# Two decode layers on one core: two more cache units kept between the layers, six places for w2, one first transfer, a result of 128 rows

## The chip, the cores and the metric

One core of a Trainium2 chip runs the whole program. The metric is the device time of one execution in microseconds, the median of a few runs. The profile is one execution taken by the hardware profiler; its times count from the span's start.

## The reference

```python
def _A_ref(x, k_cache, v_cache, wq, wo):      # attention of one token, 32 heads, 4096 keys, head size 128
    q = (x @ wq).reshape(B, Sq, H, Dh)
    scores = einsum("bhqd,bhkd->bhqk", q, k_cache) * (Dh ** -0.5)
    p = softmax(scores)
    o = einsum("bhqk,bhkd->bhqd", p, v_cache)
    return o.reshape(B, Sq, H * Dh) @ wo
def _B_ref(x, w1, b1, w2, b2):                # 512 -> 1376 -> 512
    return gelu(x @ w1 + b1) @ w2 + b2
for _ in range(2):                            # the same weights and caches both times
    x = x + _A_ref(layernorm(x), k_cache, v_cache, wq, wo)
    x = x + _B_ref(layernorm(x), w1, b1, w2, b2)
```

Everything is float32. K and V are 64 MiB each, far more than the core's own memory, so each layer reads nearly all of them again.

## The kernel before

The 32 heads go in 8 groups of 4. A group's K is a block of 8 MiB (8 chunks of 1 MiB, `NC` = 2048 columns on 128 partitions), and so is its V. A unit `U` is 512 columns, 256 KB; four units make a chunk. Group g is written below as K0 to K7 and V0 to V7. Layer 0 takes the groups 0 to 7, layer 1 takes them 7 to 0, so K7 and V7 are still there when layer 1 begins, and so are parts of V6.

One tile, `arena`, holds everything that is loaded. Places in it are columns worked out by hand: three blocks in turn, then `SPARE` (8 units, over V6's chunks 5 and 6), `HELD` (w1), and `PAIR` (two chunks: a group's wo and the next group's wq). All loads are issued by SP through `load` (L85 to L88) in program order, one after the other; a load whose place is still read waits there, and all loads behind it wait too. The transfers themselves run in that order.

For each group: `queries` (L211) makes q from wq on VectorE and TensorE, `scores` (L230) are 32 products a group over K, `softmax` (L235) uses VectorE, ScalarE and TensorE, and V is weighted either by products on TensorE (`values`, L260) or on ScalarE and VectorE (`weighted_by_act`, `weighted`). `late_sum` and `late_out` put a group's last sums (L283) and its wo product (L309, L311) behind the fifth chunk of the next group's scores. `idle` (L437) is a product whose result nobody reads.

Between the layers stands `mlp` (L335). In layer 0 it multiplies with w2, eleven units, in eight places of `SPARE` (`W2_AT[0]`, c modulo 8). As products free the places, `follow` (L622 to L627) issues more loads from inside the loop at c = 3, 5, 7 and 9: the rest of w2, wq of group 6, and the first units of K6. The last quarter of that goes out at L637, and K6's second chunk at L451 in two halves, behind the products of `query_block` (L197) that read the place. In layer 1, n = 1 loads the rest of K6 over K7 as K7's chunks have been used (L480), then what of V6 is not there (L482); n = 1 also asks for six of K5's eight chunks over V7 and `SPARE` (L518).

Of V6, chunks 0 to 4 stay where they are, and six units more (`KEPT`) are saved in layer 0: five in PSUM (`pK`, copied at L540 and back at L484) and one in `pB` (L606, back at L506). n_kept at L481 is the first column of V6 that has to be loaded again.

Of the kernel before, what the change touches and what calls it, by code (L numbers as in the profile page):

```python
# [28 lines left out]
KEPT = 6  # L29

# [11 lines left out]
K2_HOME = 12 * NC  # L42

V1_HOME = *(2 * BLOCK + NC * c for c in range(5)), 8 * NC, 6 * NC, 7 * NC
W2_AT = tuple(SPARE + U * (c % 8) for c in range(FB)), tuple(U * c for c in range(FB))
# [15 lines left out]
def decode_layers(ctx: ExitStack, tc: tile.TileContext, k, v, w, w1, w2, out):  # L61
# [33 lines left out]

    def of_w(first, n):

        row, i = first
        return w[row][:, AHEAD + NC * i : AHEAD + NC * (i + n)]
# [7 lines left out]
    def free_now(layer, n):  # L107

        if layer == 0:
            at = HELD + 2 * NC  # L110
        elif n == 0:
            at = 6 * NC
            return arena[:, at : at + U], arena[:, 11 * NC : 11 * NC + 4 * 129]
        else:
            at = 9 * NC if n == 1 else 14 * NC
# [14 lines left out]
    row, _ = wq_at(0)  # L130
    ahead = load(HELD, w[row][:, : AHEAD + NC])
    wq_first = chunk(ahead[:, AHEAD:])

# [77 lines left out]
    def queries(n, xc, wt, at, t=None, short=False, between=None):  # L211
        t = wt[:, 0, :] if t is None else t
        pin(nc.vector.tensor_scalar(t, wt[:, 0, :], xc[:, 0:1], None, op0=ALU.mult))
        for c in range(1, 4):
            pin(nc.vector.scalar_tensor_tensor(t, wt[:, c, :], xc[:, c : c + 1], t, op0=ALU.mult, op1=ALU.add))  # L215
# [14 lines left out]
    def scores(z, c, kt):  # L230
        for j in range(J):
            pin(nc.tensor.matmul(pS[32 * j : 32 * j + C, :], z[:, j, C - 1 - c : 2 * C - 1 - c],  # L232
                                 kt[:, j, :], start=(c == 0), stop=(c == C - 1)))
# [206 lines left out]
    for layer in range(2):  # L440
# [9 lines left out]
        if layer == 1:  # L450
            for a in (0, NC // 2):  # L451
                load(PAIR + NC + a, part(k, order[1], 1, 2)[:, a : a + NC // 2])
            here["k", order[1], 1] = chunk(arena[:, PAIR + NC : PAIR + 2 * NC])
# [10 lines left out]
        for n, g in enumerate(order):  # L464
# [35 lines left out]
            if first or final:  # L500
                for _ in range(FILL if layer == 1 else 0):
# [51 lines left out]
            if layer == 1 and n == 0:  # L553
# [46 lines left out]
            if n == G - 2:  # L600

                row = arena[:, HELD - U : HELD] if layer == 0 else p
# [16 lines left out]
        if layer == 0:  # L619
            first_k, next_wq = part(k, G - 2, 0, 1), of_w(wq_at(G - 2), 1)  # L620
            follow = {
                3: (*((W2_AT[0][a], w2[:, U * a : U * b]) for a, b in W2_PARTS[0][3:]),  # L622
                    (SPARE + NC - U, first_k[:, NC - U :])),
                5: ((SPARE + NC, next_wq[:, : 2 * U]),),
                7: ((SPARE + NC + 2 * U, next_wq[:, 2 * U :]),),
                9: ((SPARE, first_k[:, : 2 * U]),),
            }  # L627
        mlp(x1, s1, w1_t, w2_t[layer], xb, *((None, last_v) if layer == 0 else (ends, None)), follow)
        if layer == 0:
# [4 lines left out]
            g = G - 2  # L634
            wq_first = wq_next
            wq_next = chunk(arena[:, SPARE + NC : SPARE + 2 * NC])
# [51 lines left out]
```

## Time and profile before

| | us |
|---|---|
| median of 3 runs | 673.32 |
| lowest and highest run | 673.31, 673.92 |
| the profiled execution: its span | 671.6 |
| the median run over that span | 1.7 |

| engine | busy us | share of the span |
|---|---|---|
| VectorE (DVE) | 407.1 | 61% |
| TensorE (PE) | 299.7 | 45% |
| ScalarE (ACT) | 215.4 | 32% |
| DMA engines, share of their time in the program's queue | | 99.1% |

The span runs from the first to the last instruction of the profiled execution. What the device's time has beyond it, 1.7 us here, is taken as the same for both kernels. The busy shares of the engines are means over stages that differ; the DMA engines are the one resource that is busy from end to end.

### The profile page before, as it was taken

The numbers are of one execution on the slowest core, as the hardware profiler recorded it, in microseconds if no ns is written. First come the engines' busy times: TensorE is split into PE (matmuls) and PEld (weight loads), VectorE is DVE, ScalarE is ACT, GpSimd is POOL, SyncE is SP. The second block draws the span as 40 slices with busy tenths as digits, with TensorE's granted clock in tenths as the row PEclk, the third lists the DMA queues.
The fourth block names the chain that finished last, engine by engine and source line by source line (L and its number), as shares of the span: only waits on it lengthen the run. The fifth ranks groups of instructions, "written<-read, shape, count | busy, mean of one in ns | idle before, by whom it ended". The sixth has DMA issues, their size and how long they took to land.

```text
span 671.6 us, 6013 instructions
## 1 busy us (share of the span) xinstructions
PE 299.7 (45%) x2236; PEld 79.7 (12%) x2236; DVE 407.1 (61%) x510; ACT 215.4 (32%) x697; POOL 5.2 (1%) x26
## 2 busy tenths in 40 slices
PE   1511703415116053165768986704316025065597
PEld 1000100101001010011114311101001001011124
DVE  3059679498696886971322313288597694973513
ACT  0047074190560823802011200083290650910010
POOL 1000000000000000000000000000000000000000
PEclk9965755757558557578689998655757559557799
DMA  9999999999999999999999999999999999999997
GB/s 377 437 437 438 435 437 437 403 461 437 437 437 397 444 426 434 433 429 426 425 415 399 422 422 438 437 433 433 431 433 437 437 430 402 462 426 414 431 414 286
DMA packets 11556, 285.29 MB, mean 425 GB/s; under 512 B 1284, under 2 KB 1288, under 8 KB 3720
## 3 DMA queue, kind: packets, MB, share of 16 engines
q1 hardware_dynamic: 11528, 284.92, 99.1%
q8 instruction: 17, 0.28, 0.2%
q14 instruction: 11, 0.09, 0.0%
HBM read 284.92 MB, written 0.00 MB: 424 GB/s over the span
## 4 chain that ended last, share of the span: by engine, by line
DMA 64%; PE 17%; DVE 15%; issue 1%; another core or an unknown queue 1%; SPq 1%; ACT 0%; DVEq 0%; ACTq 0%
DMA arena<-in_v 37%; DMA arena<-in_k 24%; PE pS L232 8%; DVE arena L274 7%; PE pO L262 5%; DMA arena<-in_w 4%; DVE arena L279 3%; DVE arena L311 2%; PE pO L283 1%; DVE arena L287 1%; DVE arena L215 1%; SPq L87 1%; PE pB L323 1%; DVE arena L309 0%
## 5 line engine op out<-in xcount | busy, mean ns | idle before, releaser
L269 ACT ACTIVATE arena<-arena,pt 128x128 f32<-128x128 f32 x640 | 188.0, 387 | 50.8 <-DMA arena<-in_v 48.1
L232 PE MATMUL pS<-arena,smalls 128*8 128x512 f32 x1024 | 147.0, 727 | 78.4 <-DMA arena<-in_k 74.3
L279 DVE TENSOR_TENSOR arena<-arena 128x4096 f32<-128x4096 f32 x30 | 132.6, 4420 | 0.3
L274 DVE TENSOR_TENSOR arena<-arena,pt 128x2048 f32<-128x2048 f32 x40 | 89.0, 2287 | 36.8 <-DMA arena<-in_v 35.7
L217 PE MATMUL pS<-arena,smalls 128*128 128x512 f32 x20 | 20.7, 1140 | 202.5 <-DVE arena L215 202.5
L244 ACT ACTIVATE arena<-pS,smalls 128x512 f32<-128x512 f32 x16 | 12.4, 777 | 289.4 <-DVE smalls L243 289.4
L287 DVE STREAM_TRANSPOSE arena<-pO 128x512 f32<-128x512 f32 x16 | 11.5, 717 | 97.4 <-PE pO L262 61.9
L262 PE MATMUL pO<-arena,pt 128*4 128x512 f32 x368 | 48.9, 666 | 11.8 <-DMA arena<-in_v 11.0
L232 PEld LDWEIGHTS pS<-arena,smalls 128*8 128x8 f32 x1024 | 29.8, 102 | 198.6 <-issue 177.3
L236 DVE TENSOR_REDUCE smalls<-pS 128x1 f32<-128x512 f32 x16 | 11.0, 687 | 64.1 <-PE pS L232 64.1
L215 DVE SCALAR_TENSOR_TENSOR arena<-arena,smalls 128x512 f32<-128x512 f32 x45 | 33.8, 752 | 1.6
L311 DVE SCALAR_TENSOR_TENSOR arena<-arena,smalls 128x512 f32<-128x512 f32 x39 | 29.3, 752 | 1.4
L217 PEld LDWEIGHTS pS<-arena,smalls 128*128 128x128 f32 x20 | 5.0, 311 | 206.2 <-DVE arena L215 206.2
L315 PE MATMUL pB<-arena,smalls 128*1 128x512 f32 x26 | 14.7, 648 | 29.0 <-DVE arena L311 29.0
L246 PE MATMUL pO<-ident,arena 128*128 128x128 f32 x64 | 13.4, 344 | 28.1 <-ACT arena L244 27.8
L574 DVE TENSOR_TENSOR arena<-arena 128x2048 f32<-128x2048 f32 x10 | 22.9, 2292 | 0.3
L382 ACT ACTIVATE smalls<-smalls 128x4 f32<-128x4 f32 (+1 forms) x6 | 1.2, 205 | 44.0 <-DVE smalls L375 25.6
L262 PEld LDWEIGHTS pO<-arena,pt 128*4 128x4 f32 x368 | 9.8, 93 | 44.8 <-issue 42.4
L250 DVE STREAM_TRANSPOSE smalls<-smalls 128x32 f32<-128x32 f32 x16 | 3.4, 212 | 17.5 <-ACT arena L244 17.5
L246 PEld LDWEIGHTS pO<-ident,arena 128*128 128x128 f32 x64 | 8.4, 167 | 42.1 <-ACT arena L244 36.7
L244 ACT ACT_TABLE_LOAD x1 | 1.3, 1283 | 36.9 <-DVE smalls L243 36.9
L438 PE MATMUL pS<-arena,ident 128*8 128x256 f32 (+1 forms) x34 | 11.9, 454 | 0.5 <-DVE pt L367 0.5
(115 smaller groups left out, 183.6 us busy)
## 6 DMA issues: line engine op xcount, KB each, us to landing
arena<-in_w SPq DMA_DIRECT2D x13, 2048.0 KB, 12.5
arena<-in_k SPq DMA_DIRECT2D x6, 4096.0 KB, 21.3
arena<-in_v SPq DMA_DIRECT2D x2, 4096.0 KB, 25.1
arena<-in_w SPq DMA_DIRECT2D x6, 1024.0 KB, 30.9
arena<-in_v SPq DMA_DIRECT2D x2, 2048.0 KB, 37.0
arena<-in_k SPq DMA_DIRECT2D x2, 2048.0 KB, 13.4
arena<-in_w SPq DMA_DIRECT2D x7, 512.0 KB, 9.3
arena<-in_v SPq DMA_DIRECT2D x3, 1024.0 KB, 46.3
```

The costliest lines, as they stand in the source:

```text
L215: pin(nc.vector.scalar_tensor_tensor(t, wt[:, c, :], xc[:, c : c + 1], t, op0=ALU.mult, op1=ALU.add))
L217: pin(nc.tensor.matmul(at, one.to_broadcast([P, P]), t, start=True, stop=True))
L232: pin(nc.tensor.matmul(pS[32 * j : 32 * j + C, :], z[:, j, C - 1 - c : 2 * C - 1 - c], kt[:, j, :], start=(c == 0), stop=(c == C - 1)))
L246: nc.tensor.transpose(pT[:, b].rearrange("p j r -> p (j r)"), p[:, P * b : P * (b + 1)], ident)
L262: nc.tensor.matmul(pO[32 * j : 32 * j + 4, :], pt[:, j, c, :], by_head(vt)[:, j], start=(i == 0), stop=(i == of - 1))
L269: nc.scalar.activation(own, own, AF.Copy, scale=pt[:, j, c, b : b + 1])
L274: nc.vector.tensor_tensor(own, own, weight, op=ALU.mult)
L279: pin(nc.vector.tensor_tensor(a, a, b, op=ALU.add))
L287: nc.vector.transpose(ot[:, :512], pO)
L311: pin(nc.vector.scalar_tensor_tensor(t, wt[:, d, :], on[:, d : d + 1], t, op0=ALU.mult, op1=ALU.add))
L315: pin(nc.tensor.matmul(pB[0:1, :], one, t, start=n == 0, stop=n == G - 2))
L574: pin(nc.vector.tensor_tensor(total, total, other, op=ALU.add))
```

## The change

- Two units more of V6 stay (`INPLACE` = 2): the last two of chunk 6, at `SPARE` + 6 and + 7 units, are not overwritten, so the load at L482 starts 512 KB later in V6. Chunk 6's first two units, which were saved in PSUM, come back to `SPARE` + 4 and + 5 units (`V1_HOME`), where all four then lie side by side.
- For that, w2 in layer 0 has six places (c modulo 6). Its parts (6, 8), (8, 10) and (10, 11) all go out from `follow`. The row of pB lies in the fifth place, and so part (4, 6), and w1's last part behind it, wait for the products that read the row (L332).
- wq of group 6 goes to the places 5, 0, 1 and 4 as four units; K6's first two units to the places 2 and 3, its next four to `PAIR` in one load, and the rest over K7 (units 6 to 10, 10 to 14, 14 to 32).
- K5's first six chunks go in one load over V7 (`K2_HOME` = 10 chunks), and `SPARE` is not needed for them.
- x, biases, wq of group 0, wo of group 0 and wq of group 1 come in one first load from an array of their own, where wo and wq of group 1 were a load behind V0.
- The result is written as 128 rows of 512 bytes instead of 4; the host takes every 32nd.
- In layer 0's last group, three idle products follow the scores and two the softmax, as they do in layer 1.

```diff
+INPLACE = 2
-K2_HOME = 12 * NC
-V1_HOME = *(2 * BLOCK + NC * c for c in range(5)), 8 * NC, 6 * NC, 7 * NC
-W2_AT = tuple(SPARE + U * (c % 8) for c in range(FB)), tuple(U * c for c in range(FB))
+K2_HOME = 10 * NC
+V1_HOME = *(2 * BLOCK + NC * c for c in range(5)), 8 * NC, SPARE + NC, 7 * NC
+W2_AT = tuple(SPARE + U * (c % 6) for c in range(FB)), tuple(U * c for c in range(FB))
...
+    def unit(t, j):
+        return t[j] if isinstance(t, list) else t[:, j, :]
+    def units(*places):
+        return [arena[:, at : at + U] for at in places]
...
         elif n == 0:
-            at = 6 * NC
-            return arena[:, at : at + U], arena[:, 11 * NC : 11 * NC + 4 * 129]
+            at, ot_at = 6 * NC + 2 * U, 9 * NC + 3 * U - 4
+            return arena[:, at : at + U], arena[:, ot_at : ot_at + 4 * 129]
...
-    row, _ = wq_at(0)
-    ahead = load(HELD, w[row][:, : AHEAD + NC])
+    ahead = load(PAIR - AHEAD - NC, start)
     wq_first = chunk(ahead[:, AHEAD:])
+    w_first = chunk(ahead[:, AHEAD + NC :]), chunk(ahead[:, AHEAD + 2 * NC :])
...
-        if layer == 1:
-            for a in (0, NC // 2):
-                load(PAIR + NC + a, part(k, order[1], 1, 2)[:, a : a + NC // 2])
-            here["k", order[1], 1] = chunk(arena[:, PAIR + NC : PAIR + 2 * NC])
+            load(PAIR + NC, k[order[1]][:, 2 * U : 6 * U])
...
-                tiles = [(c, here["k", g, c]) for c in range(2)]
-                tiles += list(stream("k", g, ((2, 3), (3, 4), (4, 8)), -2 * NC))
-                n_kept = STAY + U * KEPT
-                load(V1_HOME[6] + n_kept % NC, v[g][:, n_kept:BLOCK])
-                for u in range(STAY, n_kept - U, U):
+                for a, b in ((6, 10), (10, 14), (14, 32)):
+                    load(U * (a - 6), k[g][:, U * a : U * b])
+                late_at = PAIR + NC
+                tiles = [(0, units(SPARE + 2 * U, SPARE + 3 * U, late_at, late_at + U)),
+                         (1, units(late_at + 2 * U, late_at + 3 * U, 0, U))]
+                tiles += [(c, chunk(arena[:, U * (4 * c - 6) : U * (4 * c - 2)])) for c in range(2, C)]
+                n_kept = STAY + U * (KEPT + INPLACE)
+                load(V1_HOME[n_kept // NC], v[g][:, n_kept:BLOCK])
+                for u in range(STAY, STAY + U * (KEPT - 1), U):
...
-                for _ in range(FILL if layer == 1 else 0):
+                for _ in range(FILL if layer == 1 or final else 0):
                     idle(t, pO)
...
-                for pieces, base in ((((0, 4),), K2_HOME), (((4, 6),), SPARE - 4 * NC)):
-                    for _ in stream("k", order[2], pieces, base):
-                        pass
+                for _ in stream("k", order[2], ((0, 6),), K2_HOME):
+                    pass
...
-                for _ in range(FILL - 1 if layer == 1 else 0):
+                for _ in range(FILL - 1):
                     idle(t, pS)
...
-            if layer == 1 and n == 0:
+            if layer == 0 and n == 0:
+                wo_t, wq_next = w_first
+            elif layer == 1 and n == 0:
...
-                    for a, b in W2_PARTS[0][1:3]:
-                        load(W2_AT[0][a], w2[:, U * a : U * b])
-                        if a == 4:
-                            load(HELD + W1_AT[2], w1[:, W1_AT[2] :])
+                    a, b = W2_PARTS[0][1]
+                    load(W2_AT[0][a], w2[:, U * a : U * b])
+                    load(HELD + W1_AT[2], w1[:, W1_AT[2] :])
...
-                row = arena[:, HELD - U : HELD] if layer == 0 else p
+                row = arena[:, SPARE + NC : SPARE + NC + U] if layer == 0 else p
...
-                3: (*((W2_AT[0][a], w2[:, U * a : U * b]) for a, b in W2_PARTS[0][3:]),
-                    (SPARE + NC - U, first_k[:, NC - U :])),
-                5: ((SPARE + NC, next_wq[:, : 2 * U]),),
-                7: ((SPARE + NC + 2 * U, next_wq[:, 2 * U :]),),
-                9: ((SPARE, first_k[:, : 2 * U]),),
+                3: (part_2, part_3),
+                5: (part_4, (SPARE + 5 * U, next_wq[:, :U])),
+                7: ((SPARE, next_wq[:, U : 3 * U]),),
+                9: ((SPARE + 2 * U, next_k[:, : 2 * U]),),
...
-            load(SPARE + 2 * U, first_k[:, 2 * U : NC - U])
+            load(SPARE + 4 * U, next_wq[:, 3 * U :])
+            wq_next = units(SPARE + 5 * U, SPARE, SPARE + U, SPARE + 4 * U)
...
-    nc.sync.dma_start(out, y[0:P:32, :])
+    nc.sync.dma_start(out, y)
```

## Rows read from the trace of the kernel before

**Rows 1.** Page: DMA share by 40 slices, bytes read, chain of waits by engine.

```profile
DMA  9999999999999999999999999999999999999997
HBM read 284.92 MB, written 0.00 MB: 424 GB/s over the span
DMA 64%; PE 17%; DVE 15%; issue 1%; another core or an unknown queue 1%; SPq 1%; ACT 0%; DVEq 0%; ACTq 0%
```

**Rows 2.** Windows: stretch, length, engines' busy us (count), PE clock, DMA share, GB/s.

```profile
0.70:1.70 1.00, 0.00 (x0) 0.00 (x0) 0.75 (x4) 0.00 (x0) 0.61 (x5) 1.00 0.00 0
...
340.00:346.00 6.00, 3.86 (x24) 0.80 (x28) 0.09 (x2) 0.45 (x2) 0.00 (x0) 0.72 0.96 404
...
352.00:360.00 8.00, 7.08 (x139) 4.09 (x142) 2.81 (x14) 0.20 (x1) 0.94 (x3) 1.00 1.00 416
...
364.00:366.00 2.00, 1.37 (x49) 0.83 (x48) 0.16 (x1) 0.00 (x0) 0.10 (x1) 1.00 1.03 404
366.00:368.00 2.00, 1.46 (x34) 0.83 (x34) 0.35 (x2) 1.55 (x3) 0.19 (x1) 1.00 1.00 357
368.00:370.00 2.00, 1.63 (x50) 0.98 (x46) 0.64 (x3) 0.14 (x1) 0.00 (x0) 1.00 0.95 336
...
420.00:650.00 230.00, 97.99 (x557) 21.76 (x560) 154.79 (x168) 81.92 (x270) 0.00 (x0) 0.66 1.00 430
```

**Rows 3.** Timeline, layer 0's start: SP's issues and VectorE (idle before, releaser).

```profile
0.72 0.40 SPq L87 DMA_DIRECT2D arena<-in_w  x1
...
11.76 0.33 SPq L87 DMA_DIRECT2D arena<-in_v  x1
...
65.58 0.69 DVE L223 TENSOR_REDUCE smalls<-arena 128x4 f32<-128x512 f32 x1
...
81.97 0.33 SPq L87 DMA_DIRECT2D arena<-in_w  x1
```

**Rows 4.** Chain of waits in order of time: start, us, what.

```profile
69.51 7.38 PE pS L232 x40
...
360.18 7.25 DMA arena<-in_w
...
371.15 7.05 PE pS L232 x64
...
414.61 24.39 DMA arena<-in_v
```

**Rows 5.** DMA issues (KB, us to landing): issued at 35.13, 364.64, 366.88, 370.48, 380.79, 408.74.

```profile
arena<-in_v SPq DMA_DIRECT2D x1, 54.3
...
arena<-in_w SPq DMA_DIRECT2D x1, 512.0 KB, 5.4
...
arena<-in_w SPq DMA_DIRECT2D x1, 512.0 KB, 4.4
...
arena<-in_k SPq DMA_DIRECT2D x1, 512.0 KB, 7.1
...
arena<-in_v SPq DMA_DIRECT2D x1, 1536.0 KB, 15.4
...
arena<-in_k SPq DMA_DIRECT2D x1, 2048.0 KB, 11.9
```

**Rows 6.** Timeline of SP between the layers: start, time from first to last issue, count.

```profile
364.64 2.57 SPq L87 DMA_DIRECT2D arena<-in_w  x2
```

**Rows 7.** Timeline, layer 1's first group: ScalarE's copy and exponential, query products.

```profile
377.38 0.59 ACT L506 COPY arena<-pB 128x512 f32<-128x512 f32 x1 [9.23 <-PE pS L232]
...
380.08 0.78 ACT L244 ACTIVATE arena<-pS,smalls 128x512 f32<-128x512 f32 x1 [2.12 <-DVE smalls L243]
...
380.69 1.05 PE L226 MATMUL pO<-smalls,arena 128*128 128x1 f32 x8
```

**Rows 8.** Timeline: products at layer 0's last V, and the result's issue.

```profile
342.14 5.04 PE L262 MATMUL pO<-arena,pt 128*4 128x512 f32 x32 [2.48 <-DMA arena<-in_v]
...
668.93 0.65 SPq L641 DMA_DIRECT2D out<-arena  x1
```

More of the change, by code (lines that the diff above doesn't have):

```diff
@@ L60, in decode_layers @@
 @with_exitstack
-def decode_layers(ctx: ExitStack, tc: tile.TileContext, k, v, w, w1, w2, out):
+def decode_layers(ctx: ExitStack, tc: tile.TileContext, k, v, w, start, w1, w2, out):
     nc = tc.nc
@@ L211, in queries @@
     def queries(n, xc, wt, at, t=None, short=False, between=None):
-        t = wt[:, 0, :] if t is None else t
-        pin(nc.vector.tensor_scalar(t, wt[:, 0, :], xc[:, 0:1], None, op0=ALU.mult))
+        t = unit(wt, 0) if t is None else t
+        pin(nc.vector.tensor_scalar(t, unit(wt, 0), xc[:, 0:1], None, op0=ALU.mult))
         for c in range(1, 4):
-            pin(nc.vector.scalar_tensor_tensor(t, wt[:, c, :], xc[:, c : c + 1], t, op0=ALU.mult, op1=ALU.add))
+            pin(nc.vector.scalar_tensor_tensor(t, unit(wt, c), xc[:, c : c + 1], t, op0=ALU.mult, op1=ALU.add))
         if short:
@@ L232, in scores @@
             pin(nc.tensor.matmul(pS[32 * j : 32 * j + C, :], z[:, j, C - 1 - c : 2 * C - 1 - c],
-                                 kt[:, j, :], start=(c == 0), stop=(c == C - 1)))
+                                 unit(kt, j), start=(c == 0), stop=(c == C - 1)))
     def softmax(sc, nsc, p, hold):
@@ L619, in decode_layers @@
         if layer == 0:
-            first_k, next_wq = part(k, G - 2, 0, 1), of_w(wq_at(G - 2), 1)
+            next_k, next_wq = k[G - 2], of_w(wq_at(G - 2), 1)
+            part_2, part_3, part_4 = ((W2_AT[0][a], w2[:, U * a : U * b]) for a, b in W2_PARTS[0][2:])
             follow = {
-                3: (*((W2_AT[0][a], w2[:, U * a : U * b]) for a, b in W2_PARTS[0][3:]),
-                    (SPARE + NC - U, first_k[:, NC - U :])),
-                5: ((SPARE + NC, next_wq[:, : 2 * U]),),
-                7: ((SPARE + NC + 2 * U, next_wq[:, 2 * U :]),),
-                9: ((SPARE, first_k[:, : 2 * U]),),
+                3: (part_2, part_3),
+                5: (part_4, (SPARE + 5 * U, next_wq[:, :U])),
+                7: ((SPARE, next_wq[:, U : 3 * U]),),
+                9: ((SPARE + 2 * U, next_k[:, : 2 * U]),),
             }
@@ L633, in decode_layers @@
             xs, s = set_x(of_32(mt, 4), 1.0, xb, True)
-            g = G - 2
             wq_first = wq_next
-            wq_next = chunk(arena[:, SPARE + NC : SPARE + 2 * NC])
-            load(SPARE + 2 * U, first_k[:, 2 * U : NC - U])
-            here["k", g, 0] = chunk(arena[:, SPARE : SPARE + NC])
+            load(SPARE + 4 * U, next_wq[:, 3 * U :])
+            wq_next = units(SPARE + 5 * U, SPARE, SPARE + U, SPARE + 4 * U)
     xb_rows, y = ends[:, P : 2 * P], ends[:, 2 * P :]
     nc.vector.tensor_tensor(y, pM, xb_rows, op=ALU.add)
-    nc.sync.dma_start(out, y[0:P:32, :])
+    nc.sync.dma_start(out, y)
 def columns(a):
@@ L660 @@
     w = np.array(w).transpose(0, 2, 1, 3).reshape(2, P, G * NC)
+    start = np.pad(np.concatenate((wq[0], wo[0], wq[1]), axis=1), ((0, 0), (AHEAD, 0)))
     w = np.pad(w, ((0, 0), (0, 0), (AHEAD, 0)))
@@ L666 @@
     ):
-        w[1, :, at : at + t.shape[1]] = t
+        start[:, at : at + t.shape[1]] = t
     arrays = dict(
@@ L671 @@
         w=w,
+        start=start,
         w1=np.concatenate([w1[..., 32 * a : 32 * b].reshape(P, -1) for a, b in HIDDEN], axis=1),
@@ L681 @@
         args.append(nc.dram_tensor(f"in_{name}", t.shape, F32, kind="ExternalInput").ap())
-    args.append(nc.dram_tensor("out", (J, P), F32, kind="ExternalOutput").ap())
+    args.append(nc.dram_tensor("out", (P, P), F32, kind="ExternalOutput").ap())
     with tile.TileContext(nc) as tc:
@@ L685 @@
     r = run_bass_kernel_spmd(nc, [feeds], core_ids=[0])
-    got = np.asarray(r.results[0]["out"])
+    got = np.asarray(r.results[0]["out"])[::32]
     return np.ascontiguousarray(got).reshape(1, 1, D)
```

## The prediction

> **What bounds the kernel now.** The page comes first: the DMA engines are busy in every slice but the last, and the chain of waits is a DMA for 64% of the span [rows 1]. The windows say how well the bytes flow: 430 GB/s over the 230 us of layer 1's steady part [rows 2]. 284.92 MB at 430 GB/s is 662.6 us of a span of 671.6. So bytes taken away count in full, wherever the queue of transfers has work on both sides of them; an engine counts only where it makes a load go out so late that the queue has run empty. There are three such places to look at: the start, the stretch between the layers (windows of 357 and 336 GB/s from 366 to 370 [rows 2], where the chain goes through products and short loads [rows 4]), and the end. How late a load may be is read from the first one: issued at 0.72 [rows 3], no byte moved before 1.70 [rows 2], so I take 1.0 to 1.3 us from an issue to its first bytes.
>
> **The bytes.** The load at L482 shrinks from 1,536 to 1,024 KB: 524,288 bytes at 430 GB/s are 1.2 us. It is worth that only if the queue stays full until the next load that waits for computing. That one is V5, issued at 414.61 when the last product of n = 1 has run [rows 4]; K5's last two chunks in front of it land at 408.74 + 11.9 = 420.6 [rows 5]. The queue then held 6.0 us, and will hold 4.8, against the 1.3 a load needs to start: the gain stands. Likewise K5's first part, which waits for n = 0's products over V7 and goes out at about 390.2 before and after: V6's rest lands at 380.79 + 15.4 = 396.2 [rows 5], now some 395.0. -1.2 us, between -1.25 and 0.
>
> **Short rows.** A load of 512 KB has rows of 4 KB, one of 1 MB rows of 8 KB. A stretch of mostly 4 KB and 2 KB rows flowed at 404 GB/s, one of mostly 8 KB rows at 416 [rows 2]. K6 has 512 KB in loads of 256 and 512 KB where it had 2,048 KB; wq's 1 MB is cut finer, so that half of it has 2 KB rows. 1.5 MB less at 404 instead of 416 GB/s is 1.57 MB x (1/404 - 1/416) = 0.11 us, and wq gives a little of it back. -0.1 us, between -0.2 and 0.
>
> **The start.** One load of 3 MB in place of 1 MB and, behind V0, 2 MB. The bytes are the same, so K1 lands when it did. V0 no longer waits for the place of the first wq (issued at 11.76 before [rows 3]), but the 8 MB of K0 were in the queue then, so this frees nothing. Rows of 24 KB instead of 8 KB can save at most 1.08 MB x (1/416 - 1/430) = 0.08 us, and the wait before the first byte is there in both: -0.1 us, between -0.3 and 0. The price is that K0 and V0 come behind 2 MB more, 2.1 MB / 430 = 4.9 us later, and with them all work of n = 0. The query of n = 1 was ready at 66.3 (L223) [rows 3] and would be at 71.1; its scores began at 69.5, when K1 landed [rows 4]. So they start 1.7 us later, and the load that waits behind them (wo and wq of the next group, through `late_sum`, L311) goes out at 83.7 instead of 81.97 [rows 3]. The transfer in front of it, V1, was issued at 35.13 and lands at 89.4 [rows 5]: 4.4 us of queue left after 1.3 us to start. It costs nothing, and from V1's landing on every step falls where it did. If that cover went, the price would be up to 1.7 us.
>
> **Between the layers.** What moves here is when places come free.
> 1. w2's part (4, 6) and w1's last part now wait for the row's products, to about 354, and (6, 8) for the products of c = 0 and 1, that is to 360.18, where (8, 10) went out before [rows 4]. SP stands still meanwhile, but nothing behind it could go. (8, 10) landed 7.25 us after 360.18 [rows 4], so the queue was that long; what is ahead of (6, 8) still ends behind 364. Nothing.
> 2. At 364.64 a wq load of 512 KB went out [rows 6]; now that place belongs to w2's last part and one wq unit, and the next 512 KB wait for c = 7, at about 366.88 as before. Up to there the queue is 512 KB, 1.2 us, thinner. The load of 364.64 landed at 370.0 and that of 366.88 at 371.3 [rows 5]. In the new order w2's last part and the wq unit end at about 368.8, and a load issued at 366.88 has its first bytes at 368.2. So the engine that comes last does not run dry; those ahead of it do, for up to 1.2 us. The windows show them near that already: a DMA share of 0.95 and 336 GB/s at 368 to 370 [rows 2]. Between 0 and +1.2, and I take 0, because a load has landed when its last engine is done, and that one has work.
> 3. K6's next four units go out in one load after the last query product, at about 370.5, when the second half of two went out [rows 5]; the first went half a us earlier. 0 to +0.5, I take 0: the load in front is by then not done.
> 4. The last part of K6 (14 to 32) needs K7's seventh chunk instead of the sixth. The eight take 7.05 us [rows 4], so one is 0.9 us later, against 2 MB ahead of it (4.9 us). Nothing.
> 5. pB's copy (L506) now goes to the unit in which the query sum lies. It ran at 377.38, ahead of the exponential at 380.08; it must now wait for the query products, 380.69 to 381.74 [rows 7]. Behind the exponential it costs nothing. If ScalarE keeps it ahead, the exponential starts at 381.74 + 0.59, 2.3 us late, and all of n = 0 and n = 1 with it. V5 would be issued at 416.9 against a queue that ends at 420.6 - 1.2 - 0.2 = 419.2: 1.0 us more than a start needs. Nothing as long as that holds.
>
> **Idle products** fill the 2.48 us in which TensorE waits for V at 342.14 [rows 8]. The granted clock was 0.72 on average from 340 to 346, part at 1.2 and part at 2.4 GHz [rows 2], so the four chunks' products (5.04 us) can be 1 to 2 us shorter; the pieces of V behind them set the pace. 0, and 0 if the three products hold up the transposes by a little, since V lands 2.5 us after these.
>
> **The result.** The issue of the 4-row form took 0.65 us on SP [rows 8], that of a 128-row load 0.40 [rows 3]: -0.25. 62 KB more at 430 GB/s are +0.15. Together -0.1, between -0.25 and +0.2. The Trainium skill (DMA: Bandwidth & Descriptors, section "Anatomy of one DMA") speaks against a gain here: most of a transfer's fixed time is the receipt of its last byte, longest from HBM, whatever the size. By that the form of the rows would give nothing, the 62 KB would cost their 0.15 us, and the time would be 672.1. No row tells the two apart, since the trace has one store.
>
> **Sum**: -1.2 - 0.1 - 0.1 - 0.1 = -1.5 us on the profiled span of 671.6, so 670.1. The median run is 1.7 above the span, and I carry that over: 673.3 - 1.5 = **671.8 us**.
>
> **The rivals.**
> - *The queue thins out between the layers.* Points 2 and 3 cost a part or all of 1.2 + 0.5 us. For it: the windows at 357 and 336 GB/s. Against: the last engine has work by the sum above. With half of it, 0.85, the time is 672.7, within 0.2%.
> - *Slower: each load of that stretch is an issue that the queue waits for.* The place is 364 to 372; the mechanism, that at 366.88 less than 1.3 us of transfers is left, so that the lateness shows in full: 2.24 us of the 512 KB of wq (364.64 to 366.88), 0.5 of K6's half, and 0.9 of the seventh chunk, 3.6 in all: 671.8 + 3.6 = 675.4. It is slower from 2.9 us lost on. Against it: the load issued at 364.64 took 5.4 us to land [rows 5], so there was work ahead.
> - *The bytes are saved where nobody waits.* If V5's issue came later than the queue's end less 1.3 us (point 5 and another 1.0 us of delay), layer 1 would start from that issue and the 1.2 us would be idle time: 673.0.
> - *More than the sum.* The stretch from 364 to 370 flowed at 404, 357 and 336 GB/s; 2 x (26 + 73 + 94) / 430 = 0.9 us are lost against 430. Fewer and longer loads may win back most: 670.9.
> - *A fixed price for each transfer.* The code has four transfers fewer (one at the start, three of K6, one of K5, against one more of wq); if each had a price of its own beside its bytes, that would be gained four times. Loads of 512 KB in a full queue landed 1.3 us apart (370.0, 371.3 [rows 5]), which is their bytes (1.2 us), so the price here is under 0.1 us each and the gain under 0.4: 671.4. The Trainium skill (DMA: Bandwidth & Descriptors, section "Anatomy of one DMA") gives some 2.0 us fixed for each DMA on the other issuing path and the advice to join loads; by that the time would be some 665, an estimate that those landings speak against.
>
> **How the numbers follow.** About 0.2%, 1.35 us, is what a measurement of this kernel can tell from no change; that bound is at 671.97, next to the forecast. Forecast (its own range 671.2 to 672.4) 0.50, of which 0.34 lie under the bound; thinner queue 0.22; saved for nobody 0.05; slower 0.08; more than the sum 0.12; fixed price 0.03. Faster 0.34 + 0.12 + 0.03 = 0.49, slower 0.08, within 0.43. The range goes from 670.8 (the gain of the fourth rival) to 673.2 (the thinner queue with 1.4 us of its 1.7 lost).
>
> **What would show it.** Right: the landing of V6's rest and of V5 in layer 1 some 1.2 us earlier, K1's landing at the start unmoved, the windows from 366 to 372 no lower. Wrong: a DMA share well under 0.95 there, V5 issued later than 416, ScalarE's L506 ahead of L244, or a longer stretch from the last product to the end.

## The result, and the profile after

The changed kernel takes **675.12 us** (median), where the kernel before takes 673.87 in runs on the same chips: a ratio of 1.0017, with a 95% interval from 1.0011 to 1.0023. That is about 1.2 us (0.0017 x 673.87) **slower**. It lies inside the 0.2% band that was called "the same", and outside the range that was given: the sign is wrong, and the upper end of 673.2 was too low. The profiled execution has a span of 673.7 us, against 671.6 before.

The page of the changed kernel, the parts that answer to [rows 1]; the first row counts TensorE's instructions, the row "q8 instruction" is the queue over which the engines' own code is loaded (transfers, MB, share):

```profile
PE 302.0 (45%) x2246; PEld 80.4 (12%) x2246; DVE 407.0 (60%) x510; ACT 215.4 (32%) x697; POOL 5.2 (1%) x26
...
DMA  9999999999999999999999999999999999999996
...
q8 instruction: 17, 0.28, 0.2%
...
HBM read 284.39 MB, written 0.07 MB: 422 GB/s over the span
```

The bytes fell as planned, 284.92 to 284.39 MB, and the rate over the span fell with them, from 424 to 422 GB/s. So look where the rate fell. The windows of the changed kernel between the layers, columns as in [rows 2]:

```profile
364.00:366.00 2.00, 1.68 (x50) 0.87 (x48) 0.00 (x0) 0.21 (x1) 0.00 (x0) 1.00 0.95 356
366.00:368.00 2.00, 1.21 (x26) 0.70 (x30) 0.51 (x2) 1.32 (x2) 0.29 (x2) 1.00 0.84 304
368.00:370.00 2.00, 1.63 (x42) 0.86 (x38) 0.64 (x3) 0.37 (x2) 0.00 (x0) 1.00 0.82 247
370.00:372.00 2.00, 1.68 (x42) 0.91 (x38) 1.04 (x8) 0.00 (x0) 0.45 (x1) 1.00 0.84 246
...
374.00:376.00 2.00, 2.00 (x24) 0.52 (x20) 1.07 (x2) 0.59 (x1) 0.00 (x0) 1.00 0.85 283
...
364.00:378.00 14.00, 12.20 (x200) 4.85 (x199) 5.05 (x19) 2.48 (x5) 0.84 (x3) 1.00 0.90 306
340.00:346.00 6.00, 5.44 (x38) 1.20 (x38) 0.45 (x3) 0.82 (x2) 0.00 (x0) 1.00 0.94 399
```

The kernel before, in windows that no row ahead shows:

```profile
370.00:372.00 2.00, 1.66 (x26) 0.65 (x21) 1.15 (x10) 0.00 (x0) 0.55 (x1) 1.00 0.98 374
...
374.00:376.00 2.00, 2.00 (x24) 0.55 (x20) 0.83 (x2) 0.00 (x0) 0.00 (x0) 1.00 1.08 412
...
364.00:378.00 14.00, 12.11 (x199) 4.83 (x199) 5.06 (x19) 2.28 (x4) 0.84 (x3) 1.00 1.01 383
```

The DMA share is 0.82 to 0.84 from 366 to 372, where it was 0.95 or more in every window of that stretch. Over the 14 us 306 instead of 383 GB/s were moved: 14 x 77 / 430 = **2.5 us** of transfers are left over. The busy times of the products are nearly the same in both (12.20 and 12.11 us), so TensorE did not get slower there.

DMA issues of the changed kernel, to be read against [rows 5] (KB, us from issue to landing): the first unit of wq issued at 365.16, its second part at 367.12, K6's 512 KB at 368.50 and its 1,024 KB at 370.75, and V6's rest at 381.03:

```profile
arena<-in_w SPq DMA_DIRECT2D x1, 256.0 KB, 3.9
...
arena<-in_w SPq DMA_DIRECT2D x1, 512.0 KB, 4.2
...
arena<-in_k SPq DMA_DIRECT2D x1, 512.0 KB, 4.8
...
arena<-in_k SPq DMA_DIRECT2D x1, 1024.0 KB, 7.6
...
arena<-in_v SPq DMA_DIRECT2D x1, 1024.0 KB, 15.8
```

512 KB are 1.2 us of transfers at 430 GB/s. The unit of wq lands at 369.0, and the 512 KB behind it at 371.4, 2.4 us later; K6's 512 KB land another 2.0 us later, at 373.3. In the kernel before, the same two loads landed 1.3 us (371.3 after 370.0 [rows 5]) and 1.5 us (372.8 after 371.3) behind the load ahead of them, so nearly by their bytes. Half-microseconds of the changed kernel show what happens between:

```profile
367.50:368.00 0.50, 0.18 (x8) 0.21 (x12) 0.00 (x0) 0.50 (x1) 0.00 (x0) 1.00 0.58 213
368.00:368.50 0.50, 0.50 (x20) 0.24 (x16) 0.00 (x0) 0.37 (x2) 0.00 (x0) 1.00 1.10 160
368.50:369.00 0.50, 0.50 (x10) 0.18 (x2) 0.08 (x1) 0.00 (x0) 0.00 (x0) 1.00 0.34 82
369.00:369.50 0.50, 0.20 (x1) 0.00 (x0) 0.43 (x3) 0.00 (x0) 0.00 (x0) 1.00 0.87 352
```

From 367.5 on the share falls to 0.58: some engines have run out of work. The first packets of the load issued at 367.12 start at 368.1, but 160 and 82 GB/s flow, and 352 only from 369.0 on. The share of 1.10 beside 160 GB/s says that packets can take long and carry little: a high DMA share alone does not show that bytes flow.

V6's rest lands at 381.03 + 15.8 = 396.8; the forecast was 395.0, and before it was 396.2. So **1.8 us** were lost ahead of it against the forecast: the 1.2 us that were saved, and 0.6 more. 0.3 of the 1.8 were there ahead of the stretch (a load of w2 that went out at 360.18 [rows 4] has its counterpart at 360.45).

The end, from the timeline of the changed kernel (start, time from the first to the last, engine, line, tiles, count, and in brackets the idle time before and what ended it):

```profile
669.26 0.95 PE L422 MATMUL pO<-arena,smalls 128*1 128x128 f32 x23 [0.22 <-DMA arena<-in_w]
...
670.51 0.27 PE L422 MATMUL pO<-arena,smalls 128*1 128x128 f32 x1 [0.30 <-issue]
...
671.14 0.35 SPq L648 DMA_DIRECT2D out<-arena  x1
```

and of the kernel before, where the result goes out at 668.93 [rows 8]:

```profile
667.59 0.96 PE L414 MATMUL pO<-arena,smalls 128*1 128x128 f32 x24 [0.22 <-DMA arena<-in_w]
```

Before, the 24 last products run as one group. After, 23 run, and the 24th comes later, released by nothing that the profile knows ("issue"). From the last weights' landing to the result's issue it is 1.37 us (671.14 less 669.77), and was 0.83 (668.93 less 668.10): **0.54 us** that no part of the prediction has.

### The profile page after: what moved, and what is told of

Same layout as the page of the kernel before. It is cut to its first block, busy times and chain, and to the rows that moved or that the text cites. A ratio compares the mean times of both kernels' runs of the same rounds, so it can differ in the third digit from the quotient of the medians.

```text
span 673.7 us, 6022 instructions
## 1 busy us (share of the span) xinstructions
PE 302.0 (45%) x2246; PEld 80.4 (12%) x2246; DVE 407.0 (60%) x510; ACT 215.4 (32%) x697; POOL 5.2 (1%) x26
## 3 DMA queue, kind: packets, MB, share of 16 engines
HBM read 284.39 MB, written 0.07 MB: 422 GB/s over the span
## 4 chain that ended last, share of the span: by engine, by line
DMA 67%; DVE 17%; PE 14%; issue 1%; SPq 1%; ACT 0%; DVEq 0%; ACTq 0%
DMA arena<-in_v 41%; DMA arena<-in_k 19%; DMA arena<-in_w 7%; DVE arena L282 7%; PE pS L240 6%; PE pO L270 5%; DVE arena L287 5%; DVE arena L319 2%; DVE arena L295 1%; PE pO L291 1%; SPq L88 1%; PE pB L331 1%; PE pO L422 0%; DVE arena L317 0%; PE pO L446 0%
## 5 line engine op out<-in xcount | busy, mean ns | idle before, releaser
L240 PE MATMUL pS<-arena,smalls 128*8 128x512 f32 x1024 | 144.6, 717 | 75.1 <-DMA arena<-in_k 67.4
L446 PE MATMUL pS<-arena,ident 128*8 128x256 f32 (+1 forms) x38 | 13.7, 469 | 0.5 <-DVE pt L375 0.5
```

## The experiments

All times are medians; each ratio is against the kernel before on the same chip, whose median was 673.35 to 673.55 there.

**One part at a time.** First the places alone: the changed kernel without the new start, the result's form and the idle products.

```
-    ahead = load(PAIR - AHEAD - NC, start)
...
+    ahead = load(HELD, w[row][:, : AHEAD + NC])
...
-                for _ in range(FILL if layer == 1 or final else 0):
+                for _ in range(FILL if layer == 1 else 0):
...
-    nc.sync.dma_start(out, y)
+    nc.sync.dma_start(out, y[0:P:32, :])
...
```

> The change without three of its parts: first transfers as before, result in 4 rows, no idle products in layer 0; only the places between the layers are new (the two units stay, w2 in six places, wq, K6 and K5 moved). Late-issue theory (the 1.2 us of V6 are given back because the queue between the layers runs empty): within 0.5 us of the kernel before, with a DMA share clearly under 0.95 between 367 and 372. Code theory (the 10 more products of the idle loops move the program's code and the last two products wait for it): the 0.5 us that the end has lengthened by are gone here. Start theory (the one first load of 24 KB rows costs 0.3 to 0.6 us): V1 lands at 89.4 again. If all three hold, 0 to -0.5 us against before; if the places alone carry the whole loss, +1.

674.37 us, ratio 1.0020 (1.0006 to 1.0033). So the places alone bring the loss, and more than the bytes give. Its products and windows show something of their own:

```profile
369.88 0.40 PE L422 MATMUL pO<-arena,smalls 128*1 128x128 f32 x8 [1.65 <-DMA arena<-in_w]
...
366.00:368.00 2.00, 1.42 (x34) 0.83 (x34) 0.40 (x2) 1.50 (x3) 0.21 (x2) 1.00 0.82 292
368.00:370.00 2.00, 0.35 (x17) 0.12 (x9) 0.00 (x0) 0.19 (x1) 0.00 (x0) 1.00 0.78 251
370.00:372.00 2.00, 1.63 (x35) 0.93 (x31) 0.64 (x3) 0.00 (x0) 0.00 (x0) 0.72 0.84 264
372.00:374.00 2.00, 1.82 (x34) 1.03 (x30) 1.14 (x8) 0.00 (x0) 0.12 (x1) 0.50 0.45 174
```

TensorE waited 1.65 us for a late load of weights, was busy for 0.35 us from 368 to 370, and then its granted clock fell from 2.4 to 1.2 GHz (0.72 on average from 370 to 372, 0.50 from 372 to 374), ahead of the products over K7 that release K6's next places. This execution's span is 676.0. The kernel's times range from 673.42 to 677.82, so a late load can be paid for twice here.

Then the bytes alone: the kernel before, with the load of V6's rest 512 KB shorter and no place taken for them.

```
-                load(V1_HOME[6] + n_kept % NC, v[g][:, n_kept:BLOCK])
+                load(V1_HOME[7], v[g][:, n_kept + 2 * U : BLOCK])
```

> The kernel before with the load of V6's rest shortened by its first 512 KB (chunk 6's last two units are left unloaded, so V6's part of the result isn't computed from them); every place and every other load as before. Bytes theory of the prediction: -1.2 us, V5's landing 1.2 us earlier. Rival (the bytes are saved where nobody waits): 0, with V5's landing unmoved since its issue at about 414.6 sets it.

672.67 us, ratio 0.9990 (0.9981 to 0.9999), -0.7 us with an interval (-1.3 to -0.1) that holds the -1.2. V5 lands at 438.3, where it landed at 440.0. So the bytes count. Between this kernel and the one above lie 0.30%, 2.0 us (some 1.1 to either side), which is the price of the places.

The idle products alone, put into the kernel before:

```
-                for _ in range(FILL if layer == 1 else 0):
+                for _ in range(FILL if layer == 1 or final else 0):
...
-                for _ in range(FILL - 1 if layer == 1 else 0):
+                for _ in range(FILL - 1):
```

> The kernel before with the idle products of layer 0's last softmax alone. Prediction: 0. Code theory: +0.5 us, all of it behind the last transfer's landing, the last products standing apart from the others by about 0.6 us; the clock from 340 to 346 rises to 1.0 and nothing before the end moves by more than 0.1.

674.57 us, ratio 1.0015 (1.0006 to 1.0023): a loss of 1.0 us from five products that fill a wait some 330 us ahead of the end. The place of the loss is the end. Its timeline:

```profile
668.14 0.95 PE L414 MATMUL pO<-arena,smalls 128*1 128x128 f32 x22 [0.19 <-DMA arena<-in_w]
...
669.82 0.38 PE L414 MATMUL pO<-arena,smalls 128*1 128x128 f32 x2 [0.72 <-issue]
...
670.55 0.66 SPq L641 DMA_DIRECT2D out<-arena  x1
```

Here two products come late, and the result goes out 1.89 us behind the last landing (668.66) instead of 0.83, 1.06 us later.

The start alone and the result alone:

```
...
+    ahead = load(PAIR - AHEAD - NC, start)
...
+    w_first = chunk(ahead[:, AHEAD + NC :]), chunk(ahead[:, AHEAD + 2 * NC :])
...
```

> The kernel before with the one first load of 3 MB alone. Prediction: -0.1 us. Start theory: K0 lands 0.6 us later than its bytes ask for (30.5 instead of 29.9), V1 0.3 us later than before, and +0.3 us stays to the end.

```
...
-    nc.sync.dma_start(out, y[0:P:32, :])
+    nc.sync.dma_start(out, y)
...
```

> The kernel before with the result in 128 rows alone. Prediction: -0.1 us (-0.25 to +0.2): the issue takes 0.35 to 0.40 instead of 0.65 us and the bytes 0.15 more. By the changed kernel's trace (issue 0.35, landing 1.56 after it, against 0.65 and 1.70): -0.14.

The start: 673.19 us, 0.9994 (0.9985 to 1.0003). The result: 673.05 us, 0.9992 (0.9983 to 1.0000). Both together in the kernel before:

> The kernel before with the one first load and the result in 128 rows, and nothing else of the change. By the two runs of these parts alone (0.9994 and 0.9992): -0.5 us, 672.9, faster than both kernels. Prediction's terms: -0.2.

673.37 us, 0.9998 (0.9989 to 1.0007). A loss at the start is not there, and neither is a gain that can be told from none.

**The end: is it the place of the idle products, or their number?** The changed kernel without its five new ones (the edit of the idle products, undone):

> The changed kernel without the idle products of layer 0's last softmax. Code theory (the products lengthen the program by 20 instructions of TensorE, so that its last ones are fetched late): the last products stand together again, 0.4 to 0.6 us are gone behind the last landing, and the time falls by 0.5 to 1.0 against the changed kernel, to 674.2 or less. Rival (the products pay for themselves by holding the clock in the stretch between the layers, which the new places have made tight): as slow or slower than the changed kernel, with wider spread, wherever the granted clock falls to half between 345 and 378.

674.47 us, 1.0012 (1.0003 to 1.0020). The last 24 products run as one group again, and it is 0.83 us from landing to issue. The time is only 0.05% below the changed kernel's, less than these intervals can tell from none, where 0.5 to 1.0 us had been expected. Then five idle products in the kernel before at quite another place, behind layer 0's first scores:

```
-                for _ in range(FILL if layer == 1 else 0):
+                for _ in range(FILL if layer == 1 else FILL + 2 if first else 0):
```

> The kernel before with five idle products more, not in layer 0's last softmax but behind the scores of its first group, where TensorE waits some 4 us for V0. Code theory: +0.8 to +1.2 us, as with the products in the last softmax, and the end's last products 0.6 to 1.0 us behind the others; the clock between the layers as before. Rival (the place of the products in the last softmax is what costs, by what they hold up there): 0, the end's products together.

674.79 us, 1.0015 (1.0006 to 1.0023), the same loss, with the same two products late:

```profile
668.09 0.95 PE L414 MATMUL pO<-arena,smalls 128*1 128x128 f32 x22 [0.23 <-DMA arena<-in_w]
...
669.49 0.38 PE L414 MATMUL pO<-arena,smalls 128*1 128x128 f32 x2 [0.45 <-issue]
```

And the changed kernel with its five in layer 0, and as many fewer in layer 1:

```
-                for _ in range(FILL if layer == 1 or final else 0):
+                for _ in range(FILL if final else 0):
...
-                for _ in range(FILL - 1):
+                for _ in range(FILL - 1 if layer == 0 else 0):
```

> The changed kernel with five idle products fewer in layer 1 (the three behind its first scores, the two ahead of its last V), so that TensorE's program is as long as before the change while the new idle products of layer 0 stay. Code theory: the end's last products stand together again, 0.8 us from the last landing to the result's issue instead of 1.4, -0.5 against the changed kernel. If the clock falls in layer 1's first softmax or at the end for want of those products, part is given back.

674.41 us, 1.0009 (1.0000 to 1.0018), and the late product is gone:

```profile
668.25 0.96 PE L422 MATMUL pO<-arena,smalls 128*1 128x128 f32 x24 [0.22 <-DMA arena<-in_w]
```

In time this is 0.08% below the changed kernel, again within the noise; what the two runs show is the end itself. So it is the number of TensorE's instructions ahead of the end that brings the late products, and not where they stand. What makes the last ones late is seen in the queue of code. Its last transfer for the changed kernel, from the view of DMA in the 0.2 us from 668.0, and for the idle products alone, in the 0.2 us from 667.2:

```profile
q8 instruction: 1, 0.02, 34.7%
```

```profile
q8 instruction: 1, 0.02, 33.8%
```

Each is one block of 16 KB on one DMA engine, in the midst of the last weights. Its packet starts at 668.12 and 667.36 and takes 1.1 us. The late products start at 670.51 and 669.82, 2.4 and 2.5 us behind that start; in the run with five products elsewhere it is 666.98 to 669.49, 2.5 us, and in the deep one below 665.30 to 667.68, 2.4 us. In the kernel before, the block starts at 667.26, and the whole group runs from 667.59, 0.3 us later: its products don't wait for that block.

If the late products wait for the block and not for the weights, they must cost less the further the block starts ahead of the last weights' landing. The seven profiled kernels with 2,246 matmuls bear that out (three of them come below; "lost" is the time from the last landing to the result's issue, less 0.83):

| run | block starts ahead of the last landing, us | lost at the end, us |
|---|---|---|
| idle products alone | 1.30 | 1.06 |
| K6 in halves (below) | 1.36 | 0.84 |
| five products elsewhere | 1.62 | 0.79 |
| deep (below) | 1.61 | 0.56 |
| changed kernel | 1.65 | 0.54 |
| units loaded again (below) | 2.00 | 0.27 |
| middle half of wq earlier (below) | 2.37 | 0.00 |

The two columns add to 2.2 to 2.4 us in every row. In the kernels with 2,236 it is 0.83 us each time, wherever the block lies. By these times the late products are the first of a new block; no row names the block to which an instruction belongs. The Trainium skill (Runtime: NRT & Kernel Launch, section "Instruction fetch mechanics") says that an engine's code comes in blocks of 16 KiB while it runs, and that the crossing of a border is mostly hidden. The size agrees with the transfers here; at the end of this kernel the crossing isn't always hidden and costs 0 to 1.1 us.

**The places: bytes in the queue, or the bytes of the program?** The changed kernel with the same 512 KB loaded once more, ahead of V6's rest, so that it saves nothing:

```
+                load(SPARE + 6 * U, v[g][:, n_kept - 2 * U : n_kept])
```

> The changed kernel, but the two kept units of V6 are loaded again (512 KB more, at n = 1 of layer 1), so all bytes of before in the new places. Bytes theory: +1.2 against the changed kernel, +2.4 against before. Rival (the kept bytes are saved where nobody waits in the new places): 0 to +0.3 against the changed kernel.

675.88 us, 1.0035 (1.0022 to 1.0047): 0.18% above the changed kernel, 1.2 us (0.3 to 2.1 by the two intervals), which is 512 KB at 430 GB/s. So bytes count there, and in full as far as this can tell.

Then the middle half of wq sent out two chunks earlier, into a place of w1:

```
-                5: (part_4, (SPARE + 5 * U, next_wq[:, :U])),
-                7: ((SPARE, next_wq[:, U : 3 * U]),),
+                5: (part_4, (SPARE + 5 * U, next_wq[:, :U]), (HELD + W1_AT[1], next_wq[:, U : 3 * U])),
...
```

> The changed kernel, but wq's middle two units (512 KB) go out at c = 5, 2.3 us earlier, into w1's second part, which is no longer needed in this layer (layer 1's MLP then has wrong weights there; its work is the same). Late-issue theory: the queue is as deep as before the change, the DMA share from 366 to 374 is back over 0.95, and 1.0 to 1.8 us of the loss between the layers return: -1.0 to -1.8 against the changed kernel, under the kernel before. Rival (once the places have moved, something else than depth slows the transfers there, or one code transfer hits the slowest engine): less than 0.4 us, rates still under 320 GB/s at 368 to 372.

673.91 us, 1.0005 (0.9996 to 1.0014); the 14 us from 364 move 348 GB/s instead of 306. Of the 0.17% lost, 0.12% is back, 0.8 us. But 0.54 us of that are the end, where this kernel has no late product:

```profile
667.84 0.96 PE L422 MATMUL pO<-arena,smalls 128*1 128x128 f32 x24 [0.22 <-DMA arena<-in_w]
```

The 0.3 us that remain for the stretch can't be told from nothing, where 1.0 to 1.8 had been expected, and V6's rest lands at 396.6, hardly earlier than in the changed kernel. The rate rose, but this run doesn't show that time came back with it.

An attempt to thin out the kernel before, the first half of wq issued with the second:

```
-                5: ((SPARE + NC, next_wq[:, : 2 * U]),),
-                7: ((SPARE + NC + 2 * U, next_wq[:, 2 * U :]),),
+                7: ((SPARE + NC, next_wq[:, : 2 * U]), (SPARE + NC + 2 * U, next_wq[:, 2 * U :])),
```

> The kernel before with one issue moved: wq's first 512 KB go out at c = 7 with the second half, at about 366.9 instead of 364.6; every place, every byte and the order of the transfers as before. Late-issue theory: the queue is 512 KB thinner in that stretch, as in the changed kernel, and this alone costs +0.8 to +1.8 us, with the DMA share from 366 to 372 falling to 0.8 to 0.9. Rival (the new places or the longer rows of the later loads slow the transfers): 0 to +0.3.

673.49 us, 0.9996 (0.9987 to 1.0005). It tells nothing: the load still went out at 364.4, since it waits for its place, which is free by then, and not for the chunk beside which it is written. With the two in the other order it does wait, behind the second half on SP's queue:

```
-                5: ((SPARE + NC, next_wq[:, : 2 * U]),),
-                7: ((SPARE + NC + 2 * U, next_wq[:, 2 * U :]),),
+                7: ((SPARE + NC + 2 * U, next_wq[:, 2 * U :]), (SPARE + NC, next_wq[:, : 2 * U])),
```

> The first of h1's two alone: wq's first half behind its second, 512 KB thinner from 364.6 to 366.9. Depth theory: about half of h1, +0.3 to +0.9. Rival: 0.

674.53 us, 1.0015 (1.0007 to 1.0024). The same, and K6's first two units besides later:

```
+            load(SPARE, first_k[:, : 2 * U])
...
-                9: ((SPARE, first_k[:, : 2 * U]),),
```

> The kernel before with two loads of 512 KB put behind later ones in SP's order, all places and bytes as before: wq's first half behind its second (so it goes out at about 367.2 instead of 364.6), K6's first two units behind its second chunk (at about 370.9 instead of 368.2). The queue is 512 KB thinner from 364.6 to 366.9 and from 368.2 to 370.9. Depth theory: DMA share at 0.8 to 0.9 and rates under 320 GB/s there, +0.8 to +1.8 us. Rival (something else in the new order): 0 to +0.3.

674.66 us, 1.0020 (1.0011 to 1.0029). These two are the kernel before with its bytes, its places and its TensorE program. Only the first half of wq goes out later (in the first of them at 367.26 for 364.64), and in the second K6's first units too. In the first, K6's loads go out as before (368.19 for 368.25), so no engine's computing was held up; only the queue was thinner. The windows of the second:

```profile
366.00:368.00 2.00, 1.65 (x43) 0.86 (x36) 0.01 (x1) 1.69 (x3) 0.00 (x0) 1.00 0.75 230
...
364.00:378.00 14.00, 12.10 (x191) 4.65 (x184) 5.23 (x20) 2.27 (x4) 0.84 (x3) 1.00 0.96 351
```

A share of 0.75 where it was 1.00 [rows 2], and 1.0 us (0.5 to 1.6) and 1.35 us (0.7 to 2.0) slower. The second delay adds nothing that can be told from noise. In the profiled execution of the first, V6's rest lands at 396.75, only 0.5 us later than before, and the last weights 1.3 us later (669.42 for 668.11); where the other 0.8 us arose is not shown. The reverse, the changed kernel with two more places (those of w1's first part, which layer 1 then lacks), so that every load goes out as early as before:

```
...
-                3: (part_2, part_3),
-                5: (part_4, (SPARE + 5 * U, next_wq[:, :U])),
-                7: ((SPARE, next_wq[:, U : 3 * U]),),
-                9: ((SPARE + 2 * U, next_k[:, : 2 * U]),),
+                3: (part_2, part_3, (HELD, part_4[1]), (HELD + U, next_wq[:, :U])),
+                5: ((SPARE + 4 * U, next_wq[:, U : 3 * U]),),
+                7: ((SPARE, next_wq[:, 3 * U :]), (SPARE + U, next_k[:, :U])),
+                9: ((SPARE + 2 * U, next_k[:, U : 3 * U]),),
...
```

> The changed kernel with two places more between the layers (w1's first part, which is then missing in layer 1's first hidden columns; the work is the same), used so that every load from 361 on goes out when its counterpart in the kernel before does; the bytes of V6 stay saved, the 128-row result, the first load and the idle products stay. Depth theory: the 1.7 us of the stretch come back, -1.5 us or more against the changed kernel (673.6 or less), the DMA share over 0.93 from 366 to 374. Rival: under 0.6 us.

672.90 us, 0.9997 (0.9988 to 1.0005): 0.20% or 1.35 us (0.6 to 2.1) below the changed kernel, with the same bytes, and with the late product still at its end (0.56 us lost there for 0.54). V6's rest lands at 394.8, where the forecast had 395.0. Its windows:

```profile
366.00:368.00 2.00, 1.53 (x34) 0.83 (x34) 0.27 (x2) 1.63 (x3) 0.19 (x1) 1.00 1.01 368
...
364.00:378.00 14.00, 12.13 (x200) 4.81 (x196) 5.05 (x19) 2.86 (x5) 0.84 (x3) 1.00 1.01 372
```

Last, K6's four units as two loads of 512 KB instead of one of 1,024:

```
-            load(PAIR + NC, k[order[1]][:, 2 * U : 6 * U])
+            for a in (0, 2):
+                load(PAIR + NC + U * a, k[order[1]][:, U * (2 + a) : U * (4 + a)])
```

> The changed kernel with K6's next four units in two loads of 512 KB, as before, so that the first goes out half a us earlier. Depth theory: a small gain, 0.1 to 0.5 us against the changed kernel. Rival (that one load with rows of 8 KB behind an empty queue is what is slow): -0.8 or more.

674.76 us, 1.0020 (1.0011 to 1.0028), no better than the changed kernel. A gain of 0.1 to 0.5 us, as expected from the half us by which the first of them goes out earlier, can be neither seen nor excluded by these intervals; the rival's 0.8 us or more is not there.

## Why the prediction was wrong

**The bytes, right.** Saving them alone gives -0.7 us (-1.3 to -0.1), loading them again costs 1.2 (0.3 to 2.1).

**Short rows, the start, the result: small, as said.** What short rows cost by themselves no run tells apart. The start's cover held: the load of wo and wq, forecast for 83.7, went out at 83.68, and V1 landed at 39.77 + 49.9 = 89.7. That is 0.3 us later than before, within what the start alone leaves open (-1.0 to +0.2 us). The issue of the 128-row form took 0.35 us instead of 0.65, and it landed 1.56 us after the start of its issue instead of 1.68 (670.61 less 668.93). By the Trainium skill's rule (DMA: Bandwidth & Descriptors, section "Anatomy of one DMA", which is written for transfers issued from GpSimd, where this one comes from SP) the form would give nothing, and 0.15 us would be lost. These landings, 0.12 us sooner with 62 KB more, speak against that. The times can't decide it: the store alone gives -0.5 us (-1.1 to 0.0), together with the start -0.1 (-0.7 to +0.5).

**Between the layers, point 2: the step that failed.** I put it between 0 and +1.2 us and took 0, because "the engine that comes last does not run dry". The readings under it were right: the loads ahead ended at 369.0 (368.8 forecast), the next one's first packets came 1.0 us after its issue (1.0 to 1.3 taken), and the 5.4 and 4.4 us of [rows 5] were a queue with work in it, since each of those loads landed 1.2 to 1.3 us behind the one ahead. What was drawn from them was wrong:
- First bytes were taken for a full flow. From 368.0 to 369.0 the flow is 160 and 82 GB/s; the packets of 4 KB that start there take some 470 ns, where they take 165 in a full queue. 352 GB/s come 1.9 us after the issue. So the load landed 2.4 us behind the one ahead of it, for 1.2 us of bytes.
- Work on the last engine was to be enough. The rates from 367.5 on say that engines which are done early stand still, and what is not moved then is moved later: of 2.5 us left over 1.8 were still there at V6's rest (0.3 of them from ahead of the stretch).
- The choice between the ends. The nearest row was the window with 0.95 and 336 GB/s, and it was named as a sign that the engines were "near that already"; the value taken was nevertheless the favourable end.

The price, where it is alone: 1.0 and 1.35 us for loads that go out later in the kernel before, 1.35 us given back by two more places in the changed one (each with 0.5 to 0.7 us to either side), and 2.0 between the places and the bytes. So the first rival had the mechanism and the size (up to 1.7 us), and I gave it a chance of 0.22 and half its price. The second rival's 3.6 us did not come.

**Point 3**: the later K6 costs nothing that the halves can show. **Point 4**: nothing of it is seen. **Point 5, right**: the copy (L515 now) stayed behind the exponential. ScalarE in the changed kernel:

```profile
380.31 0.78 ACT L252 ACTIVATE arena<-pS,smalls 128x512 f32<-128x512 f32 x1 [4.54 <-DVE smalls L251]
...
382.02 0.59 ACT L515 COPY arena<-pB 128x512 f32<-128x512 f32 x1 [0.84 <-PE pO L234]
```

**The idle products: a term that was costed at nothing and cost something, far from where it was looked for.** At their own place they do what was said: the granted clock from 340 to 346 is 1.00 instead of 0.72, the four chunks' products take 3.62 us instead of 5.04, and V sets the pace. What I left out is that they make TensorE's program 20 instructions longer: five products are 10 more matmuls (2,246 against 2,236) and as many weight loads. By the times of the code transfers, that moved a border of 16 KB into the last products: +1.0 us alone, 0.54 us on the end of the changed kernel. The prediction asked that "a longer stretch from the last product to the end" be looked for, but named no cause for one.

**The sum of the profiled runs** closes: V6's rest is 1.8 us behind the forecast, and the span should have been 670.1. The end lost 0.54, and the result's store gave the 0.1 that had been counted (1.56 for 1.68 us). That is 670.1 + 1.8 + 0.54 = 672.4. The profiled span is 673.7, and the remaining 1.3 us are one event but for 0.1: the load of wo and wq issued at 397.16 landed at 417.5, 6.1 us behind K5's first part instead of 4.9, and V5 at 441.8, 3.0 us behind the 438.8 that the forecast gives. It is seen in some executions of several kernels (the changed one, its version without idle products, both with idle products in the kernel before, the thinned one) and not in others. This load lands in sixteen parts, one for each DMA engine. Put in order beside those of K5's first part, fifteen come 4.9 us behind them, and one that was due at 415.9 comes at 417.45. So a single engine was held up. A block of code starts at 412.34 and takes 1.0 us on one engine; in the kernel before, one starts at 413.64 in the same load, and there the last part is not late. That the block held up the engine that then landed last would fit, but the trace doesn't name the engine, and it stays open. In the ratio of the medians there is less than in these two spans: +1.2 us.

**What stays open** beside that: why the first packets on engines that had run dry take so long. And the parts don't add up to better than some tenths: places +1.35, idle products +1.0, start and result together -0.13 give +2.2 us, where +1.2 was measured; each has an interval of 0.6 us or more to either side, and the end loses 0.54 us in the changed kernel instead of 1.06. No version that does the whole work came out clearly below the kernel before: the result's form alone is nearest to it (0.9983 to 1.0000).

## What to carry to other kernels

Memory that is kept resident is taken from the depth of the load queue: where loads wait for places, count how much of the queue is left at the thinnest point, on the engine that is done first and not on the one that is done last, and set it against the time from an issue until the bytes flow again (1.9 us to 352 GB/s here) and not to the first bytes (1.0 us). Read the rate beside the DMA share, which can be high while little flows. When a row gives a cost a range from nothing to its full price, and the nearest window already shows idle engines, take the price. Idle or additional instructions are not free because they fill a wait: look at the last instructions of the program after every change in their number, and at the last transfers of code ahead of them.

## What the runs showed of the hardware

- Into a queue that had run thin, a load's first packets came 1.0 us after its issue, and 352 GB/s only after 1.9 us (issue at 367.12 in the changed kernel). The packets of 4 KB took some 470 ns at 368 to 369, where they take 165 in a full queue. From 368.0 to 368.5 the DMA share was 1.10 at 160 GB/s.
- In the thinnest windows of 2 us 230 to 247 GB/s flow at DMA shares of 0.75 to 0.84 (the thinned and the changed kernel). A share of 0.84 of 430 GB/s would be 361, so the engines that count as busy are slower, too.
- Code comes in blocks of 16 KB, each some 1.1 us on one DMA engine amid the data. The late products at the end run 2.4 to 2.5 us after such a transfer starts, in six kernels alike. That costs up to 1.1 us, and nothing where the transfer starts 2.4 us ahead of the last weights' landing. Five products anywhere ahead can bring it about or take it away.
- After TensorE had waited 1.65 us for weights, its granted clock fell from 2.4 to 1.2 GHz within the next products in one execution (the places alone, from 370.9), and the span was the longest of all profiles.
